# Attention, a routed MoE and a dense layer in one kernel: squares and gate work moved to other places in the queues, two buffers of local queries and keys

## The chip, the cores and the metric

One core of a Trainium2 chip runs the whole program. Its engines work through queues of their own, strictly in order: TensorE (PE in the profile, its weight loads PEld), VectorE (DVE), ScalarE (ACT), GpSimd (POOL), and SyncE (SP), which issues most DMAs. An instruction that waits for another engine holds up everything behind it in its own queue. The metric is device time in microseconds (us); three runs of the kernel before took 641.94, 642.94 and 644.06, and 642.94 is their median.

## The reference, cut to what matters

Attention over 4 batches, 8 heads, 576 positions and 64 channels, then a mixture of 8 experts on the 2304 rows, then a dense layer with three up-projections and their maximum.

```python
# heads 0..3: local (0 <= rel < 32); heads 4..7: strided (same position modulo 32, rel >= 0)
scores = np.where(masks, scale * q @ k.T, -1e9)
attn = np.exp(scores - scores.max(-1)); attn /= attn.sum(-1) + 1e-9
x = (attn @ v) as rows of 512
xn = x / (norm(x) + 1e-6); en = emb / (norm(emb) + 1e-6)
logits = xn @ en.T / tau
expert_idx = argmax(logits)
gate_w = softmax(logits)[expert_idx]
out[mask] = gate_w[mask] * (relu(x[mask] @ w1[e]) @ w2[e])      # for each expert e
h = max(x @ w1, x @ w2, x @ w3); return h @ w_out
```

The expert of a row follows from the products with the normed embeddings alone, so it can be found without the norm of the row. The norm enters only in the gate weight, which is multiplied in at the very end of the kernel.

## The kernel before, in words

The program has an attention stage, then the experts one after the other, then the dense layer in blocks of 768 rows. The change touches the attention stage and its hand-over to the first expert.

**Steps of attention.** A batch is cut into six groups (`GRP`): k = 0, 1, 2 are strided heads (8, 8 and 6 softmax columns), k = 3, 4, 5 are local heads (8, 8 and 2 columns). The loop in `attention` runs over steps s; step s masks and scores group s, takes maximum and exponentials of group s-1, normalises group s-2, transposes group s-3 and multiplies group s-4 by V. So the step after a group with k = 5 has 2 exponentials and the others have 6 or 8. For a group: `g_max` (L390 on VectorE, and L394, the scaled negative maximum `nb`, on GpSimd), `g_exp` (L405, one ACTIVATE for each column on ScalarE), `g_sum` (L414, GpSimd), `g_norm` (reciprocal `ri` L420 on VectorE, then the multiplication of `p` L421 on GpSimd), `g_trans` (transposes L432, copy `pt`), `g_av` (product `x` L457 into the one PSUM buffer `x`, whose copy `xt` is put into the list `later` and emitted at the start of the next step, on ScalarE for strided and on VectorE for local heads). `tok_half` (L492) turns `xt` into rows of 128 tokens, copies them (`row`) and writes them to `x_scr`.

**Routing of a unit of tokens.** The 18 tiles of 128 tokens are routed in units of 4, 5, 4, 2 and 3 tiles. `route_stages` gives each unit's stages: `square` (L530, one ScalarE instruction for each tile: sum of squares), `logits` (VectorE, which expert), `rank` (TensorE) and `slots`, `onehots`, `tokens`, `sums` (VectorE, place in the expert's list), and `norm` (GpSimd, L546 and L547), `gate` and `gate2` (softmax of the logits: two GpSimd instructions, an exponential `pr` on ScalarE, small VectorE work). The stages go through the list `todo`, from which up to TP = 4 are emitted at the end of each step. The last unit runs `order`, which counts, sorts the experts by load and forms `win_i`, the row numbers that each expert gathers. The stages of the last two units that only the gate needs are emitted after `order` (the list `late`).

**Hand-over.** `gather(0)` (L833) is emitted after all of attention: three indirect DMAs on GpSimd fetch the rows of the first expert from `x_scr`. Two weight tiles are then split on ScalarE and VectorE (L168, L173), the gathered rows are transposed on TensorE (L862), split (`xw`, L844 and L845), and the first expert's products start (L869).

**Queues.** SyncE issues the loads of queries, keys and values of the next batch (`load_kq`, `load_v`) at fixed steps, the writes to `x_scr`, and the first two pieces `c` of the dense layer's weights (`c_load`, at steps S0 and S0 + 1). Local queries and keys (`ql`, `kl`) have one buffer.

Of the kernel before, what the change touches and what calls it, by code (L numbers as in the profile page):

```python
# [9 lines left out]
F32 = mybir.dt.float32  # L10
# [12 lines left out]
SCALE = 0.125  # L23
# [8 lines left out]
CA = 0  # L32
S0 = 13
NSTAGE = 3
NMORE = 40
CL = 0
CS = 1
E1 = 2
NA = 4
# [14 lines left out]
PSR = 2  # L54
TP = 4
W0 = 4
# [8 lines left out]
def kernel(ctx, tc, a, out, x_scr, w_scr, u_scr, perm_scr, gate_scr, upto="all"):  # L65
# [218 lines left out]
    v_p = actx.enter_context(tc.tile_pool(name="v", bufs=2))  # L284
    p_p = actx.enter_context(tc.tile_pool(name="p", bufs=LT + 1))
    pt_p = actx.enter_context(tc.tile_pool(name="pt", bufs=LA - LT + 3))
    st_p = actx.enter_context(tc.tile_pool(name="st", bufs=LA + 3))
# [31 lines left out]
    def load_kq(b, kind, cuts=None):  # L319

        for n0, n1 in cuts or ((0, S),):
            if kind:
                for t, x in zip(qk_s[::-1], ("kts", "qs")):
                    nc.sync.dma_start(
                        out=t[b % 2][:, 0:2 * S].rearrange("p (c n) -> p c n", c=2)[:, :, n0:n1], in_=a[x][b][:, :, n0:n1])
            else:
                nc.sync.dma_start(out=kl, in_=a["ktl"][b])
                nc.sync.dma_start(out=ql, in_=a["ql"][b])

# [18 lines left out]
    st = {}  # L348
    later, later_v = [], []

# [15 lines left out]
    def g_scores(g):  # L366

        b, kind, bl = group(g)  # L370
        ps, (ns, nk) = st[g]["ps"], shape(g)
        for i in range(ns):
            blk, c = bl[i // 2], i % 2
            for u in range(1 if kind else 2):
                for h in range(2):
                    r = slice(64 * h, 64 * h + 64)
                    if kind:
                        o = S * c + 54 * blk
                        q, k, p0 = qk_s[0][b % 2][r, o:o + 64], qk_s[1][b % 2][r, o:o + 54], 64 * h
                    else:  # L380
                        o = 64 * blk + 32 * u
                        q, k, p0 = ql[r, c, o:o + 32], kl[r, c, o:o + 64], 64 * u + 32 * h
                    nc.tensor.matmul(  # L383
                        out=ps[p0:p0 + q.shape[-1], nk * i:nk * i + nk], lhsT=q, rhs=k, start=False, stop=i == ns - 1,
                        skip_group_check=True)

    def g_max(g):
# [54 lines left out]
    def g_av(g):  # L442
# [38 lines left out]
    def tok_half(i, kind):  # L481
# [15 lines left out]
        if q not in rows:  # L497
            rows[q] = row_p.tile([128, 3 if q == 4 else 5, 4, 136], F32, tag=f"row{q // 4}", name="row", bufs=2 - q // 4)
        dst = rows[q][:, i - t0, 2 * kind:2 * kind + 2, :]
# [16 lines left out]
    def route_stages(b):  # L516
# [61 lines left out]
        def tokens():  # L578
# [88 lines left out]

        sq = [(0, lambda t=t: square(t)) for t in range(T)]
        if b < 3:
            return (sq[:-1] + [(0, logits)] + sq[-1:] + [(0, norm), (1, rank), (0, gate), (0, slots), (0, gate2), (0, onehots)]  # L670
                    + [(1, tokens), (0, sums)])
        rest = sq + [(0, f) for f in (norm, gate, gate2)]
        if b == 3:
            late.extend(rest)
            return [(0, f) for f in (logits, rank, sums, slots, onehots, tokens)]
        return [(0, f) for f in (logits, order)] + late + rest

    def setup():
# [5 lines left out]
        for t in qk_s[0] + qk_s[1]:  # L684
            nc.gpsimd.memset(t[:, 2 * S:NP], 0.0)
        for i in range(LT + 1):
            nc.gpsimd.memset(new_p()[:, :, 54:64], 0.0)
# [32 lines left out]

    late = []

    def attention():
        toks, todo = [], []
        last, seen, routed = [0], [0], [0]

        def next_tok():
            if toks:
                f = toks.pop(0)
                f()  # L730

        for s in range(NG + LA + 1):
# [6 lines left out]
            if 0 <= s - 1 < NG:  # L739
                g_max(s - 1)  # L740
                g_exp(s - 1)
            if 0 <= s - LN < NG:
                g_norm(s - LN)
# [9 lines left out]
            if 0 <= s - LA < NG:  # L753
# [5 lines left out]
                while k >= NS and 128 * seen[0] + 128 <= end:  # L759
# [3 lines left out]
                    if seen[0] == t0 + T:  # L763
                        toks.append(lambda q=routed[0]: todo.extend(route_stages(q)))
                        routed[0] += 1
# [4 lines left out]
            if s < NG:  # L770
                b, k = divmod(s, NB_)
                if b + 1 < B:
                    if k == 0:
                        load_kq(b + 1, 1)
                    if k == 2:
                        load_v(b + 1, 1)
                    if k == 4:
                        load_v(b + 1, 0)
                    if k == 5:
                        load_kq(b + 1, 0)  # L780
            if s in (S0, S0 + 1):
                c_load()
            if 4 < s < NG:
                now[0] += 4500
                c_after()
                if c_n[0] < CA:
                    c_before()
            for _ in range(TP):
                if todo and s >= last[0] + todo[0][0]:
                    todo.pop(0)[1]()  # L790
                    last[0] = s
        while toks:
            next_tok()
            flush(later_v)
        while todo:
            todo.pop(0)[1]()

# [22 lines left out]
    yt = [yt_p.tile([128, YT], F32, name=f"yt{c}") for c in range(4)]  # L820
    xg, xw, hh_t = {}, {}, {}

    def wins(e):
        return [(i, min(128, CAPS[e] - 128 * i)) for i in range(-(-CAPS[e] // 128))]

    def gather(e):
        t = xg_p.tile([128, 3, DM], F32, tag="xg", name="xg")
        t = [t[:, i, :] for i in range(3)]
        if len(wins(e)) > 3:
            assert e == 0  # L830
            t.append(h_p.tile([128, 2 * HB], F32, tag="h7", name="x3")[:, 0:DM])
        for i, r in wins(e):
            nc.gpsimd.indirect_dma_start(  # L833
                out=t[i][:r], out_offset=None, in_=x_scr,
                in_offset=bass.IndirectOffsetOnAxis(ap=win_i[:r, NWIN * e + i:NWIN * e + i + 1], axis=0))
        xg[e] = t

    def xw_tiles(n):
# [204 lines left out]

    gather(0)
    usable[0] = NRING
# [377 lines left out]
```

## Time and profile before

| What | us |
|---|---|
| median of three runs | 642.94 |
| the profiled execution, its own time | 647.8 |
| span of its trace | 646.0 |
| start of the first expert's products | 139.58 |
| PE busy in the span | 601.2 (93%) |
| DVE, ACT, POOL busy | 417.2, 323.5, 133.3 |

Up to 139.58 the trace is attention, routing and the hand-over; all that follows is the same in both kernels. A share of busy time over the whole span says little on this first part: there the slices of the profile have PE at 4 to 8 tenths, with its granted clock (PEclk) between 4 and 9 tenths of full speed. TensorE has two clock levels, 1.2 and 2.4 GHz; a granted clock of 0.50 in a stretch is the lower, 1.00 the higher.

### The profile page before, as it was taken

How to read it: one execution, taken by the hardware profiler on the slowest of the kernel's cores; microseconds unless marked ns; L12 is line 12 of the kernel's file. 1: busy time of each engine (PE TensorE's matmuls, PEld its weight loads, DVE VectorE, ACT ScalarE, POOL GpSimd, SP SyncE). 2: the span in 40 equal slices, each digit the busy share in tenths (PEclk: the TensorE clock that was granted, in tenths of full speed). 3: DMA queues.
4: the chain of work that ended last, by engine and by line, in shares of the span. 5: the costliest groups of instructions: out<-in, count | busy, mean ns of one | idle time of the engine just before them, and what ended most of it. 6: DMA issues, size and time to landing. Idle time of an engine off the chain costs nothing.

```text
span 646.0 us, 13803 instructions
## 1 busy us (share of the span) xinstructions
PE 601.2 (93%) x5320; PEld 564.0 (87%) x5321; DVE 417.2 (65%) x885; ACT 323.5 (50%) x905; POOL 133.3 (21%) x183
## 2 busy tenths in 40 slices
PE   7878886679999999999998999999999999999995
PEld 5767775469999999999998999988999988999984
DVE  2556574446989797979898878777354376334440
ACT  4684764234756567656765634536412246221242
POOL 2343432247414241422210000002100002000011
PEclk8787898579999999999999899999999999999998
DMA  8955721266797786868775685951177301367111
GB/s 292 381 193 211 233 68 48 101 212 205 243 355 264 259 278 245 299 207 274 266 241 179 256 330 180 333 221 66 56 268 266 126 17 66 135 252 268 47 50 53
DMA packets 44183, 129.93 MB, mean 201 GB/s; under 512 B 4400, under 2 KB 15024, under 8 KB 40912
## 3 DMA queue, kind: packets, MB, share of 16 engines
q1 hardware_dynamic: 41088, 119.50, 52.3%
q0 software_dynamic: 3024, 9.49, 4.0%
q8 instruction: 44, 0.72, 0.5%
q14 instruction: 27, 0.22, 0.1%
HBM read 96.73 MB, written 32.24 MB: 200 GB/s over the span
## 4 chain that ended last, share of the span: by engine, by line
PE 79%; DVE 7%; ACT 5%; DMA 5%; issue 2%; SPq 1%; POOL 1%; POOLq 0%; DVEq 0%; ACTq 0%
PE g L869 57%; PE q L869 10%; PE r L492 3%; PE x L457 2%; PE s L383 2%; ACT p L405 2%; DMA stage<-w 2%; ACT junk L530 1%; PE q L852 1%; DMA em<-emb 1%; DVE w L173 1%; DMA out<-r,perm_i 1%; PE t L432 1%; DVE h L889 1%; DMA xg<-x_scr,win_i 1%
## 5 line engine op out<-in xcount | busy, mean ns | idle before, releaser
L869 PE MATMUL g<-xc,w 128*128 128x384 f32 x1134 | 198.0, 335 | 0.0
L869 PEld LDWEIGHTS g<-xc,w 128*128 128x128 f32 x1134 | 196.5, 188 | 1.2 <-ACT yt L1167 0.5
L173 DVE TENSOR_TENSOR w<-stage,w 128x1024 fp32r<-128x1024 f32 x76 | 104.7, 1394 | 16.2 <-ACT w L168 15.8
L869 PE MATMUL g<-h,w 128*128 128x376 f32 (+7 forms) x768 | 113.6, 304 | 1.6 <-DVE h L889 1.6
L869 PEld LDWEIGHTS g<-h,w 128*128 128x128 f32 x768 | 106.4, 192 | 2.8 <-DVE h L889 2.2
L869 PE MATMUL g<-xw,w 128*128 128x376 f32 (+7 forms) x768 | 106.0, 298 | 0.4 <-ACT xw L844 0.3
L869 PEld LDWEIGHTS g<-xw,w 128*128 128x128 f32 x768 | 104.3, 189 | 0.9 <-ACT xw L844 0.5
L168 ACT ACTIVATE w<-stage 128x1024 fp32r<-128x1024 f32 x76 | 78.6, 1055 | 5.4 <-DMA stage<-w 4.7
L1218 POOL DMA_INDIRECT out<-r,perm_i x18 | 18.2, 1010 | 281.5 <-ACT r L1217 186.1
L869 PE MATMUL q<-w,hs 128*128 128x512 f32 x324 | 74.9, 391 | 1.3 <-DVE hs L1206 1.3
L869 PEld LDWEIGHTS q<-w,hs 128*128 128x128 f32 x324 | 60.6, 188 | 14.8 <-DVE hs L1206 2.6
L405 ACT ACTIVATE p<-s,nb 128x54 f32<-128x54 f32 (+1 forms) x160 | 46.9, 317 | 30.8 <-POOL nb L394 30.8
L244 POOL TENSOR_TENSOR f<-f,c 128x512 int32<-128x512 int32 x24 | 34.9, 1456 | 108.6 <-DVE f L242 97.1
L1167 ACT ACTIVATE yt<-g 128x384 f32<-128x384 f32 x27 | 13.3, 491 | 72.8 <-PE g L869 47.3
L1154 DVE TENSOR_TENSOR tmp<-g,yt 128x384 f32<-128x384 f32 x36 | 20.0, 556 | 44.7 <-PE g L869 44.7
L888 ACT ACTIVATE h<-g 128x376 fp32r<-128x376 f32 (+7 forms) x64 | 25.7, 411 | 29.8 <-PE g L869 27.6
L405 ACT ACTIVATION_READ_ACCUMULATOR p<-s,nb 128x1 f32 x160 | 34.2, 214 | 0.0
L903 ACT ACTIVATE yt<-g 128x376 f32<-128x376 f32 (+7 forms) x32 | 13.2, 413 | 38.7 <-PE g L869 38.7
L1007 DVE TENSOR_TENSOR xc<-yt,xc 128x384 fp32r<-128x384 f32 x42 | 21.4, 554 | 16.5 <-ACT xc L1006 16.5
L457 PEld LDWEIGHTS x<-pt,v 64*64 64x64 f32 (+2 forms) x928 | 17.4, 147 | 16.4 <-ACT xt L468 12.3
L457 PE MATMUL x<-pt,v 64*64 64x32 f32 (+2 forms) x928 | 20.4, 234 | 12.0 <-ACT xt L468 10.6
L833 POOL DMA_INDIRECT xg<-x_scr,win_i x22 | 26.0, 1181 | 24.8 <-PE q L983 11.5
(181 smaller groups left out, 725.8 us busy)
## 6 DMA issues: line engine op xcount, KB each, us to landing
stage<-w SPq DMA_DIRECT2D x64, 512.0 KB, 5.2
c<-wm SPq DMA_DIRECT2D x24, 512.0 KB, 6.2
w<-u_scr SPq DMA_DIRECT2D x12, 1024.0 KB, 4.8
u_scr<-w SPq DMA_DIRECT2D x9, 1024.0 KB, 7.7
w<-u_scr SPq DMA_DIRECT2D x12, 768.0 KB, 6.5
u_scr<-w SPq DMA_DIRECT2D x9, 768.0 KB, 10.1
w_scr<-f SPq DMA_DIRECT2D x24, 256.0 KB, 5.2
stage<-w_scr SPq DMA_DIRECT2D x12, 512.0 KB, 4.3
```

The costliest lines, as they stand in the source:

```text
L168: nc.scalar.activation(out=ws[i][:, 0, 0:m], in_=x, func=ACTF.Copy)
L173: nc.vector.tensor_tensor(out=ws[i][:, 1, 0:m], in0=x, in1=ws[i][:, 0, 0:m].bitcast(F32), op=ALU.subtract)
L244: nc.gpsimd.tensor_tensor(out=f, in0=f, in1=low, op=ALU.add)
L405: nc.scalar.activation(out=p[:, i, :nk], in_=st[g]["ps"][:, i * nk:(i + 1) * nk], func=ACTF.Exp, bias=st[g]["nb"][:, i:i + 1], scale=SCALE ...
L457: nc.tensor.matmul(out=xp[64 * h:64 * h + 64, c, o:o + n], lhsT=lhsT, rhs=rhs, start=True, stop=True)
L492: nc.tensor.matmul(out=psv[p0:p0 + n, c, :], lhsT=xT[b, kind][:, c, off:off + n], rhs=rhs_i[:, 2 * kind + c, :], start=True, stop=True)
L833: nc.gpsimd.indirect_dma_start(out=t[i][:r], out_offset=None, in_=x_scr, in_offset=bass.IndirectOffsetOnAxis(ap=win_i[:r, NWIN * e + i:NWI ...
L869: nc.tensor.matmul(out=ps, lhsT=ws(i), rhs=xs(j), start=first and n == 0, stop=last and n == 2, skip_group_check=more)
L888: nc.scalar.activation(out=h[:, 0], in_=ps, func=ACTF.Relu)
L1007: nc.vector.tensor_tensor(out=x[:, 1], in0=src[c], in1=x[:, 0].bitcast(F32), op=ALU.subtract)
L1154: nc.vector.tensor_tensor(out=tmps[i], in0=ps, in1=s, op=ALU.add)
L1218: nc.gpsimd.indirect_dma_start(out=out, out_offset=bass.IndirectOffsetOnAxis(ap=perm_i[:, col:col + 1], axis=0), in_=r, in_offset=None)
```

## The change

- The unit list becomes 4, 5, 4 and 5 tiles.
- `square` leaves `todo`. It goes into a new list `aside`, from which squares are emitted only at the end of steps with s modulo 6 equal to 0 (three), 2 (one) and 3 (two), and only while s < 24. `norm`, `gate` and `gate2` follow there one per step. `todo` gives one stage per step.
- `gather(0)` is emitted inside `attention`, after the stages in `todo` and ahead of what is left in `aside`: four squares, norm, gate and gate2 of the third unit, five squares and the same of the fourth.
- `nb`, both instructions of `gate` (df) and `tokens`' product w_tok move from GpSimd to VectorE.
- `xt` copies of local heads are emitted behind the maximum, `nb` and exponentials of the step (list `later_d`).
- `ql` and `kl` get two buffers and are loaded at k = 1 in place of k = 5; strided values at k = 1 in place of k = 2. `p` has three buffers (was 4) and `pt` three (was 4).
- The first two `c` loads are emitted at steps 20 and 21 (was 13 and 14); the embedding's norm one step later.

```diff
-S0 = 13
+S0 = 20
-E1 = 2
+E1 = 3
-TP = 4
+TP = 1
...
-    ql = pa.tile([128, 2, S], F32, name="ql")
-    kl = pa.tile([128, 2, S + 32], F32, name="kl")
+    qk_l = [[pa.tile([128, 2, n], F32, name=f"{x}{u}") for u in range(2)] for x, n in (("ql", S), ("kl", S + 32))]
...
-        nc.gpsimd.tensor_scalar(out=nb[:, 0:ns], in0=mx[:, 0:ns], scalar1=SCALE, scalar2=None, op0=ALU.mult)
+        nc.vector.tensor_scalar(out=nb[:, 0:ns], in0=mx[:, 0:ns], scalar1=SCALE, scalar2=None, op0=ALU.mult)
...
-            later.append(lambda: nc.vector.tensor_copy(out=dst, in_=src))
+            later_d.append(lambda: nc.vector.tensor_copy(out=dst, in_=src))
...
-    units = ((0, 4), (4, 5), (9, 4), (13, 2), (15, 3))
+    units = ((0, 4), (4, 5), (9, 4), (13, 5))
...
-            (nc.gpsimd if b < 4 else nc.vector).tensor_tensor(
+            nc.vector.tensor_tensor(
                 out=w_tok[:, t0:t0 + T], in0=bc(bt.unsqueeze(2), n4), in1=bc(tk.unsqueeze(3), n4), op=ALU.mult)
...
-            nc.gpsimd.tensor_tensor(out=df, in0=d["l"], in1=bc(d["mx"], s8), op=ALU.subtract)
-            nc.gpsimd.tensor_tensor(out=df, in0=df, in1=bc(rn, s8), op=ALU.mult)
+            nc.vector.tensor_tensor(out=df, in0=d["l"], in1=bc(d["mx"], s8), op=ALU.subtract)
+            nc.vector.tensor_tensor(out=df, in0=df, in1=bc(rn, s8), op=ALU.mult)
...
-        sq = [(0, lambda t=t: square(t)) for t in range(T)]
-        if b < 3:
-            return (sq[:-1] + [(0, logits)] + sq[-1:] + [(0, norm), (1, rank), (0, gate), (0, slots), (0, gate2), (0, onehots)]
-                    + [(1, tokens), (0, sums)])
-        rest = sq + [(0, f) for f in (norm, gate, gate2)]
-        if b == 3:
-            late.extend(rest)
-            return [(0, f) for f in (logits, rank, sums, slots, onehots, tokens)]
-        return [(0, f) for f in (logits, order)] + late + rest
+        sq = [lambda t=t: square(t) for t in range(T)]
+        if b < B - 1:
+            return [logits, lambda: (rank(), slots()), onehots, lambda: (tokens(), sums())], sq, [norm, gate, gate2]
+        return [logits, order], sq, [norm, gate, gate2]
...
+    SQ = {0: 3, 2: 1, 3: 2}
...
+        def route(q):
+            now_, squares, gates = route_stages(q)
+            todo.extend(now_)
+            aside.extend([(1, f) for f in squares] + [(0, f) for f in gates])
...
-            for _ in range(TP):
-                if todo and s >= last[0] + todo[0][0]:
-                    todo.pop(0)[1]()
-                    last[0] = s
+            if aside and not aside[0][0]:
+                aside.pop(0)[1]()
+            elif s < NG:
+                for _ in range(SQ.get(s % NB_, 0)):
+                    if aside and aside[0][0]:
+                        aside.pop(0)[1]()
+            if todo and routed[0] < B:
+                todo.pop(0)()
         while toks:
             next_tok()
             flush(later_v)
-        while todo:
-            todo.pop(0)[1]()
+        for f in todo:
+            f()
+        gather(0)
+        for _, f in aside:
+            f()
```

**ScalarE, end of batch 2 and start of batch 3** (p: exponentials of a group's columns; xt: copy of the product with V; junk: a square). Before:

```order
L405 ACTIVATE p,rs<-s,nb 128x64 x8
L468 ACTIVATE xt<-x 128x36x12
L405 ACTIVATE p,rs<-s,nb 128x64 x2
L530 ACTIVATE junk,ssq<-row 128x512 x4
L468 ACTIVATE xt<-x 128x36x8
L405 ACTIVATE p,rs<-s,nb 128x54 x8
L530 ACTIVATE junk,ssq<-row 128x512
```

Now, at the same place:

```order
L404 ACTIVATE p,rs<-s,nb 128x64 x8
L467 ACTIVATE xt<-x 128x36x12
L404 ACTIVATE p,rs<-s,nb 128x64 x2
L529 ACTIVATE junk,ssq<-row 128x512 x3
L467 ACTIVATE xt<-x 128x36x8
L404 ACTIVATE p,rs<-s,nb 128x54 x16
L529 ACTIVATE junk,ssq<-row 128x512
```

Three squares in place of four stand ahead of the batch's third xt copy, and the fourth stands two groups of exponentials later instead of one.

**ScalarE, from the last xt copy of attention to the first expert** (pr: the gate's exponential; w: upper half of a weight tile; xw: upper half of the gathered rows). Before:

```order
L465 ACTIVATE xt<-x 128x64
L502 ACTIVATE row<-r 128x272
L530 ACTIVATE junk,ssq<-row 128x512 x2
L591 ACTIVATE pr<-df 128x16
L530 ACTIVATE junk,ssq<-row 128x512 x3
L591 ACTIVATE pr<-df 128x24
L168 ACTIVATE w<-stage 128x1024 x2
L844 ACTIVATE xw<-g 128x376 x4
```

Now:

```order
L464 ACTIVATE xt<-x 128x64
L529 ACTIVATE junk,ssq<-row 128x512 x4
L590 ACTIVATE pr<-df 128x32
L529 ACTIVATE junk,ssq<-row 128x512 x5
L590 ACTIVATE pr<-df 128x40
L168 ACTIVATE w<-stage 128x1024 x2
L847 ACTIVATE xw<-g 128x376 x4
```

Nine squares stand here in place of five, still ahead of the first weight split, and each pr still stands between them.

**GpSimd, the same stretch** (r: sums plus 1e-9; xg: an indirect DMA of the gather; nrm and nr: the norm). Before:

```order
L583 TENSOR_TENSOR w_tok<-bt,cf 128x96
L546 TENSOR_TENSOR nrm<-ssq,ca 128x2
L547 TENSOR_SCALAR nr_2298<-nrm 128x2
L589 TENSOR_TENSOR df<-l,mx 128x16
L590 TENSOR_TENSOR df<-df,rn 128x16
L546 TENSOR_TENSOR nrm<-ssq,ca 128x3
L547 TENSOR_SCALAR nr_2318<-nrm 128x3
L589 TENSOR_TENSOR df<-l,mx 128x24
L590 TENSOR_TENSOR df<-df,rn 128x24
L833 DMA xg<-x_scr,win_i 128x512 x2
L833 DMA xg<-x_scr,win_i 120x512
```

Now:

```order
L420 TENSOR_TENSOR p<-p,ri 128x128
L725 DMA xg<-x_scr,win_i 128x512 x2
L725 DMA xg<-x_scr,win_i 120x512
L545 TENSOR_TENSOR nrm<-ssq,ca 128x4
L546 TENSOR_SCALAR nr_2257<-nrm 128x4
L545 TENSOR_TENSOR nrm<-ssq,ca 128x5
L546 TENSOR_SCALAR nr_2279<-nrm 128x5
```

The three gathers now stand ahead of both norms, and the norms behind the gathers.

## Rows read from the trace of the kernel before

**Rows 1.** Busy time by stage: start:end, length, each engine (instructions), PEclk, DMA, GB/s.

```profile
22.55:42.22 19.67, 19.45 (x524) 17.30 (x524) 12.79 (x33) 12.53 (x77) 7.38 (x18) 0.86 0.65 233
42.22:70.11 27.89, 22.56 (x550) 19.33 (x544) 15.94 (x49) 16.84 (x99) 10.36 (x24) 0.82 0.64 230
70.11:95.41 25.30, 20.53 (x534) 18.10 (x530) 16.31 (x51) 16.73 (x95) 10.32 (x23) 0.87 0.46 153
95.41:117.05 21.64, 14.06 (x233) 11.21 (x234) 9.15 (x37) 9.96 (x37) 4.38 (x10) 0.76 0.16 48
117.05:139.58 22.53, 13.06 (x79) 9.76 (x78) 10.12 (x46) 5.51 (x14) 7.05 (x16) 0.63 0.38 127
139.58:646.00 506.42, 495.70 (x3087) 476.24 (x3087) 347.00 (x656) 248.76 (x515) 86.25 (x66) 0.99 0.58 205
```

**Rows 2.** Waits from 15 to 110 us: total, times, longest.

```profile
ACT p L405 <- POOL nb L394: 26.7, 18, 3.9
PE x L457 <- ACT xt L468: 10.6, 6, 3.4
```

**Rows 3.** Timeline around a batch's end: start, us, instruction, [idle before <-releaser].

```profile
72.62 0.62 ACT L530 ACTIVATE junk<-row 128x512 f32<-128x512 f32 x1
...
75.51 0.39 ACT L468 ACTIVATE xt<-x 128x288 f32<-128x288 f32 x1
...
75.95 2.18 PE L492 MATMUL r<-rhs_i,xt 128*128 128x136 f32 x8 [1.91 <-ACT xt L468]
...
78.53 0.43 DVE L536 TENSOR_REDUCE l<-row 128x40 f32<-128x160 f32 x1
...
78.88 1.20 POOL L546 TENSOR_TENSOR nrm<-ssq,ca 128x5 f32<-128x5 f32 x1 [4.22 <-ACT junk L530]
...
79.92 0.20 DVE L542 TENSOR_TENSOR oh_all<-v,vm 128x40 bf16<-128x40 f32 x1
```

**Rows 4.** Busy time by stage, five microseconds after a wait of TensorE.

```profile
46.69:51.69 5.00, 5.00 (x70) 4.08 (x70) 1.37 (x3) 2.84 (x17) 2.31 (x6) 0.50 1.02 410
```

**Rows 5.** Timeline of the third group's maximum and nb.

```profile
11.78 0.50 DVE L390 TENSOR_REDUCE mx<-s 128x6 f32<-128x324 f32 x1 [0.65 <-PE s L383]
...
14.18 0.25 POOL L394 TENSOR_SCALAR nb<-mx 128x6 f32<-128x6 f32 x1
```

**Rows 6.** Timeline from the end of attention to the first expert.

```profile
99.33 0.88 PE L457 MATMUL x<-pt,v 54*64 54x54 f32 x24 [3.27 <-ACT xt L468]
...
113.45 0.20 PE L554 MATMUL rk<-oh_all,cb 128*128 128x16 bf16 x1 [2.58 <-DVE oh_all L542]
...
116.61 0.44 DVE L504 COPY row<-r 128x272 f32<-128x272 f32 x1 [3.21 <-PE r L492]
...
123.15 0.18 DVE L663 TENSOR_REDUCE win_i<-wp 128x3 int32<-128x24 f32 x1
...
128.71 0.22 ACT L591 ACTIVATE pr<-df 128x24 f32<-128x24 f32 x1 [1.91 <-POOL df L590]
128.84 1.99 ACT L168 ACTIVATE w<-stage 128x1024 fp32r<-128x1024 f32 x2
...
129.54 1.24 POOL L833 DMA_INDIRECT xg<-x_scr,win_i  x1 [0.86 <-issue]
...
132.36 1.00 POOL L833 DMA_INDIRECT xg<-x_scr,win_i  x1 [0.30 <-issue]
...
138.46 1.61 ACT L844 ACTIVATE xw<-g 128x376 fp32r<-128x376 f32 x4 [7.63 <-PE g L862]
```

**Rows 7.** Timeline: small VectorE work beside a GpSimd instruction, and without one.

```profile
111.66 0.51 POOL L583 TENSOR_TENSOR w_tok<-bt,cf 128x192 bf16<-128x192 f32 x1 [5.31 <-DVE bt L580]
111.73 0.46 DVE L606 TENSOR_TENSOR coh<-coh,ohs 128x8 bf16<-128x8 bf16 x1
...
117.16 0.17 DVE L606 TENSOR_TENSOR coh<-coh,ohs 128x8 bf16<-128x8 bf16 x1
```

**Rows 8.** Instructions by line, 0 to 110 us: count, busy, mean ns, idle before.

```profile
L421 POOL TENSOR_TENSOR p<-p,ri 128x432 f32<-128x432 f32 (+3 forms) x24 | 20.1, 839 | 0.8 <-DVE ri L420 0.3
```

More of the change, by code (lines that the diff above doesn't have):

```diff
@@ L284 @@
     v_p = actx.enter_context(tc.tile_pool(name="v", bufs=2))
-    p_p = actx.enter_context(tc.tile_pool(name="p", bufs=LT + 1))
-    pt_p = actx.enter_context(tc.tile_pool(name="pt", bufs=LA - LT + 3))
+    p_p = actx.enter_context(tc.tile_pool(name="p", bufs=LT))
+    pt_p = actx.enter_context(tc.tile_pool(name="pt", bufs=LA - LT + 2))
     st_p = actx.enter_context(tc.tile_pool(name="st", bufs=LA + 3))
@@ L326, in load_kq @@
             else:
-                nc.sync.dma_start(out=kl, in_=a["ktl"][b])
-                nc.sync.dma_start(out=ql, in_=a["ql"][b])
+                for t, x in zip(qk_l[::-1], ("ktl", "ql")):
+                    nc.sync.dma_start(out=t[b % 2], in_=a[x][b])
     def load_v(b, kind):
@@ L348 @@
     st = {}
-    later, later_v = [], []
+    later, later_d, later_v = [], [], []
     def flush(fs):
@@ L381, in g_scores @@
                         o = 64 * blk + 32 * u
-                        q, k, p0 = ql[r, c, o:o + 32], kl[r, c, o:o + 64], 64 * u + 32 * h
+                        q, k, p0 = qk_l[0][b % 2][r, c, o:o + 32], qk_l[1][b % 2][r, c, o:o + 64], 64 * u + 32 * h
                     nc.tensor.matmul(
@@ L497, in tok_half @@
         if q not in rows:
-            rows[q] = row_p.tile([128, 3 if q == 4 else 5, 4, 136], F32, tag=f"row{q // 4}", name="row", bufs=2 - q // 4)
+            rows[q] = row_p.tile([128, 5, 4, 136], F32, tag="row", name="row")
         dst = rows[q][:, i - t0, 2 * kind:2 * kind + 2, :]
@@ L685, in setup @@
             nc.gpsimd.memset(t[:, 2 * S:NP], 0.0)
-        for i in range(LT + 1):
+        for i in range(LT):
             nc.gpsimd.memset(new_p()[:, :, 54:64], 0.0)
@@ L719, in embed3, with wins, gather @@
         nc.vector.tensor_copy(out=rhs_i[:, :, 0:128], in_=bc(ident.unsqueeze(1), [128, 4, 128]))
-    late = []
+    xg, xw, hh_t = {}, {}, {}
+    def wins(e):
+        return [(i, min(128, CAPS[e] - 128 * i)) for i in range(-(-CAPS[e] // 128))]
+    def gather(e):
+        t = xg_p.tile([128, 3, DM], F32, tag="xg", name="xg")
+        t = [t[:, i, :] for i in range(3)]
+        assert len(wins(e)) <= 3
+        for i, r in wins(e):
+            nc.gpsimd.indirect_dma_start(
+                out=t[i][:r], out_offset=None, in_=x_scr,
+                in_offset=bass.IndirectOffsetOnAxis(ap=win_i[:r, NWIN * e + i:NWIN * e + i + 1], axis=0))
+        xg[e] = t
+    SQ = {0: 3, 2: 1, 3: 2}
     def attention():
-        toks, todo = [], []
-        last, seen, routed = [0], [0], [0]
+        toks, todo, aside = [], [], []
+        seen, routed = [0], [0]
         def next_tok():
             if toks:
-                f = toks.pop(0)
-                f()
+                toks.pop(0)()
+        def route(q):
+            now_, squares, gates = route_stages(q)
+            todo.extend(now_)
+            aside.extend([(1, f) for f in squares] + [(0, f) for f in gates])
         for s in range(NG + LA + 1):
@@ L741, in attention @@
                 g_exp(s - 1)
+            flush(later_d)
             if 0 <= s - LN < NG:
@@ L763, in attention @@
                     if seen[0] == t0 + T:
-                        toks.append(lambda q=routed[0]: todo.extend(route_stages(q)))
+                        toks.append(lambda q=routed[0]: route(q))
                         routed[0] += 1
@@ L774, in attention @@
                         load_kq(b + 1, 1)
-                    if k == 2:
+                    if k == 1:
+                        load_kq(b + 1, 0)
                         load_v(b + 1, 1)
@@ L778, in attention @@
                         load_v(b + 1, 0)
-                    if k == 5:
-                        load_kq(b + 1, 0)
             if s in (S0, S0 + 1):
@@ L820 @@
     yt = [yt_p.tile([128, YT], F32, name=f"yt{c}") for c in range(4)]
[L821 to L836, printed above, removed]
     def xw_tiles(n):
@@ L1041 @@
     perm_todo += [lambda i=i: perm_part(i) for i in range(NPT)]
-    gather(0)
     usable[0] = NRING
```

## The prediction

> **What bounds the kernel now.** I read the busy times by stage first, because the page's shares mix stages with different limits. The last stage, from 139.58 on, has TensorE busy 495.70 of 506.42 us at clock 0.99 [rows 1]; the order of instructions there is the same in both kernels, so I leave it as it is, and the question is only when it starts. Of the four batches of attention the second (22.55 to 42.22) has no routing beside it: 19.67 us, TensorE busy 19.45. The third and fourth carry the routing of the units before them and take 27.89 and 25.30, with TensorE busy 22.56 and 20.53. So a step of attention is bound by TensorE when nothing disturbs it, and routing costs 8.2 and 5.6 us a batch.
>
> Next I read the waits, for what disturbs it: ScalarE's exponentials wait 26.7 us for `nb` from GpSimd, and TensorE's product x waits 10.6 us for the xt copy on ScalarE, 3.4 at the longest [rows 2]. The timeline shows how that arises: four squares run from 72.62 until the third strided copy starts at 75.51, 0.72 us each, and TensorE stands 1.91 us at 75.95 until it has ended [rows 3]. Such a wait costs more than itself. The five microseconds after another one (46.69 to 51.69) have a granted clock of 0.50, the lower level, with TensorE busy throughout [rows 4]; at the upper level the same work would take half, so a wait of this kind costs about 2.5 us on top.
>
> Last I read the hand-over. The last row copy ends at 116.61 + 0.44 = 117.05, which I call T. The first expert's window is known at 123.33 (T + 6.28), but the first gather starts only at 129.54, because GpSimd's queue holds both norms and df ahead of it, and these wait for squares. The third gather starts at 132.36, and the xw split at 138.46; the experts start at T + 22.5 [rows 1, 6].
>
> **The change, part by part.** All against the profiled execution: 647.8 us, span 646.0 and 1.8 around it. That is 4.9 above the median of the runs, which I take off at the end.
>
> *nb on VectorE.* Removed: 24 instructions on GpSimd and, more important, their place in its queue behind r, which waits for the exponentials of the group before. The third group's maximum ended at 12.28 and its nb started at 14.18 [rows 5], so ScalarE lost 1.9 us there. Behind the maximum on VectorE nb follows at once; I price it like the smallest VectorE instruction shown, 0.17 us [rows 7], 4 us over 24 groups. It is hidden where TensorE bounds (VectorE is busy 12.79 of 19.67 in the undisturbed batch). In the first two batches I take a gain of 2 us, one such stall; the ends are 0 (TensorE or the loads bound instead) and 4 (two).
>
> *Squares, routing and xt copies.* In the third and fourth batch three squares, not four, stand ahead of the third xt copy (2.2 us instead of 2.9), behind two exponentials that no longer wait for GpSimd. I lay the engines side by side for that place: logits on VectorE (1.59 us from 78.53 to the end of oh_all [rows 3]) hold up the maximum behind them, so the two exponentials and the three squares end about 1.3 us after TensorE could use the copy. A batch is then 19.67, plus this 1.3, plus about 1 us for the step in which VectorE has onehots or tokens on top of its maximum, copies and rows: 22. The 19.67 holds one stretch at the lower clock already (mean 0.86). Two batches at 22 against 27.89 + 25.30 give 9.2. Bounds: 19.7 each (13.8 gained), and 25 each, near the faster of the two as they are (3.2 gained). I take 22, nearer to the undisturbed batch, as the squares are what TensorE waited for.
>
> *The rest of attention, 95.41 to T: 21.64 us, TensorE busy 14.06 at clock 0.76* [rows 1]. Gone: the 3.27 us in which x at 99.33 waits for a copy behind squares (those of the third unit now run after T), and the 2.58 us in which the rank of the unit of two tiles waits for VectorE at 113.45, ahead of the last two row products [rows 6]. Its clock share says that about half of the 14.06 ran at the lower level, so TensorE's work is 11 us if it stays warm, and it still waits for copies of x and rows, some 2.6 us. That makes 13.6, a gain of 8; bounds 5 (only the two waits go) and 10 (no wait left).
>
> *T to the experts.* The unit of two tiles no longer stands between T and `order`, but the last unit has five tiles: logits as above 1.59 us, and more rows in the one-hots. I get the first window at T + 5.65, 0.6 earlier. The gathers start there, at about T + 6.0. But ScalarE's queue has two pr ahead of the weight splits, and these now hang on norms that stand behind the gathers. Counted on: three gathers until T + 9.8 (129.54 to 133.36 took 3.8); norm of four tiles 1.4; three small VectorE instructions 0.7; pr 0.2, so T + 12.1. Then five squares at 0.75: T + 15.85. The norm of five tiles (1.20 and its second instruction, 1.55 in all [rows 3]): T + 17.4. VectorE 0.7, pr 0.2: T + 18.3. Two weight splits on ScalarE, 1.99 [rows 6]: T + 20.3; VectorE follows them, then the split of xw: the experts start at T + 22.3. The gather comes more than 6 us earlier and the start 0.2. Four of the nine squares are hidden (they run while GpSimd waits for the window); the other five are not. And TensorE, which before had transposes and warming products until just before the start, now has nothing from about T + 14.6 until T + 20.8, and starts cold: 2.5 us by the price above, bounds 0 and 4.
>
> *The rest at nothing.* The second buffer of local queries and keys frees SyncE's queue, but no wait of TensorE for a load stands among the waits that I read; if the loads come in a worse order early, it costs up to 1 us in the first batch. Fewer p and pt buffers: the transposes that free them come ahead of the scores that the next exponentials need. The c loads move within a stretch where DMA is at 0.16 to 0.46 [rows 1], and are used long after. df and w_tok on VectorE: within the microsecond above.
>
> Sum: 2 + 9.2 + 8 + 0.2 - 2.5 = 16.9. 647.8 - 16.9 = 630.9; less 4.9, 626.
>
> **A rule against the change.** coh, a VectorE instruction on 8 columns, takes 0.46 us beside w_tok on GpSimd, which it outlasts by a hair, and 0.17 with GpSimd idle [rows 7]. So a small VectorE instruction can be held until GpSimd is done. The Trainium skill, SBUF — State Buffer, section "SBUF: two separate sides", says that the two share one port pair, which whoever comes first keeps for a whole instruction; by that rule, and the rows agree, nb, df and w_tok can be held on VectorE.
>
> **Rivals.**
>
> *The gather ends last (617).* If the gate chain were hidden, the experts would start as they do now after the third gather: 6.1 us from it to xw [rows 6] and 1.1 more, so T + 6.0 + 2.8 + 7.2 = T + 16.0, and warm. That is 9 us earlier. Against it: the order puts both pr ahead of the weight splits. Chance 0.08.
>
> *The stalls only move (637).* VectorE becomes the bound of a step, batches stay at 25 and the rest of attention gains 5: 0 + 3.2 + 5 + 0.2 - 2.5 = 5.9. For it: VectorE is busy 16.31 of 25.30 and gets nb and df on top; against it: its time was not what TensorE waited for. Chance 0.21.
>
> *Nothing that can be measured (641 to 645, that is within 0.3%, about what tells a change from none here).* The attention gains little and the cold start takes it back. Chance 0.04.
>
> *Slower (652): the xt copy of local heads behind maximum and nb.* TensorE's product needs the one x buffer; the copy now starts some 0.9 us later. If TensorE waits over a microsecond for it, the lower clock follows as above. Nine copies at 0.9 + 2 are 26 us, against 16.9 gained. It decides from about six such waits on. Against it: mask, transposes and row products stand between in TensorE's queue. Chance 0.03.
>
> *Slower by held nb (651).* If each of 24 nb waited out GpSimd's product with p, 0.84 us on average [rows 8], with that instruction's copies behind it, some 25 us come back. That product is emitted behind the reciprocal and so behind the nb of its step, and should have ended a step later. This is what the rule of the Trainium skill would make of it. Chance 0.02.
>
> **How the numbers follow.** Forecast 0.62, at 626, by itself 620 to 633. The range 617 to 637 adds the early gather and the moved stalls up to their value. Faster by over 0.3%: 0.62 + 0.08 + 0.21 = 0.91; within 0.3% 0.04; slower 0.05.
>
> **What would show it.** Right: no ScalarE wait for nb over 2 us; squares behind two exponentials and batches of about 22 us; the experts start near 120 us (139.58 less 19.4), with the last gather landed some 9 us before; in ScalarE's queue norm, five squares, norm and pr just ahead of the first weight split; the lower clock in the first microseconds of the experts. Wrong: batches of 25 us, VectorE never idle in them, or x waiting for xt on VectorE; or an experts' stage that is not 506 us long.

## The result, and the profile after

The changed kernel takes 636.07 us (median of 13 runs, 634.11 to 641.13); the kernel before took 644.06 beside it (641.9 to 647.56). The ratio is 0.9881, 95% interval 0.9856 to 0.9905: faster by 8.0 us. The forecast was 626, so 16.9 from the median of 642.94. The time lies inside the range, 10 us above the forecast.

The profiled execution after took 634.37 us, its span is 632.5. Here are the busy times by stage after, cut where the rows of before were cut [rows 1]: second, third and fourth batch, rest of attention up to the last row copy (T), hand-over, experts and dense layer. Columns: stretch and length, then busy time and count of PE, PEld, DVE, ACT and POOL, granted clock, DMA share, GB/s.

```profile
20.20:42.98 22.78, 19.89 (x535) 17.49 (x528) 13.22 (x37) 13.12 (x83) 6.02 (x12) 0.93 0.78 295
42.98:67.24 24.26, 19.68 (x550) 16.63 (x544) 17.59 (x60) 17.36 (x102) 8.62 (x15) 1.00 0.63 224
67.24:88.26 21.02, 17.49 (x536) 15.28 (x530) 16.99 (x55) 16.50 (x94) 8.00 (x15) 1.00 0.52 168
88.26:104.03 15.77, 12.43 (x231) 10.28 (x232) 9.32 (x35) 6.90 (x27) 1.91 (x4) 0.89 0.17 50
104.03:125.93 21.90, 11.15 (x83) 8.35 (x82) 10.07 (x42) 8.87 (x23) 9.67 (x13) 0.78 0.48 164
125.93:632.50 506.57, 496.25 (x3087) 476.40 (x3087) 346.09 (x656) 247.77 (x513) 82.23 (x64) 0.99 0.57 204
```

T comes 13.0 us earlier than in [rows 1], and the experts start 13.65 earlier: nearly all of the gain lies in the attention, and the hand-over (21.90 against 22.53) and the rest (506.57 against 506.42) are about as long as before. So the spans of the two profiled executions differ by 13.5 us and the medians by 8.0. That gap of 5.5 is the first thing to explain.

The chain of the hand-over after, from its timeline (start, length, engine, line, operation; in brackets the idle time before and what ended it), to be held against [rows 6]:

```profile
103.59 0.44 DVE L503 COPY row<-r 128x272 f32<-128x272 f32 x1 [0.59 <-PE r L491]
109.52 0.18 DVE L662 TENSOR_REDUCE win_i<-wp 128x3 int32<-128x24 f32 x1
110.00 1.24 POOL L725 DMA_INDIRECT xg<-x_scr,win_i  x1 [16.68 <-DVE wp L658]
115.77 0.23 ACT L590 ACTIVATE pr<-df 128x32 f32<-128x32 f32 x1 [10.16 <-DVE df L589]
115.91 0.61 ACT L529 ACTIVATE junk<-row 128x512 f32<-128x512 f32 x1
119.72 1.19 POOL L545 TENSOR_TENSOR nrm<-ssq,ca 128x5 f32<-128x5 f32 x1 [4.49 <-ACT junk L529]
121.84 0.24 ACT L590 ACTIVATE pr<-df 128x40 f32<-128x40 f32 x1 [2.20 <-DVE df L589]
121.98 1.99 ACT L168 ACTIVATE w<-stage 128x1024 fp32r<-128x1024 f32 x2
117.38 0.57 PE L865 MATMUL g<-cf,xg 120*128 120x120 f32 x4
124.39 0.68 PE L872 MATMUL g<-xw,w 128*128 128x376 f32 x1 [6.44 <-ACT xw L847]
```

The gather starts at T + 6.0, the last transposes are over at 117.95, and then TensorE waits 6.44 us for the split of xw. That split stands behind the weight splits in ScalarE's queue, and these stand behind the second pr; ScalarE had idled 10.16 us ahead of the first pr.

### The profile page after: what moved, and what is told of

Its sections match the earlier page's. It is cut to its first block, busy times and chain, and to the rows that moved or that the text cites. A ratio compares the mean times of both kernels' runs of the same rounds, so it can differ in the third digit from the quotient of the medians.

```text
span 632.5 us, 13808 instructions
## 1 busy us (share of the span) xinstructions
PE 594.1 (94%) x5321; PEld 557.6 (88%) x5322; DVE 419.8 (66%) x901; ACT 322.7 (51%) x904; POOL 122.0 (19%) x142
## 4 chain that ended last, share of the span: by engine, by line
PE 83%; DVE 7%; ACT 4%; issue 2%; DMA 2%; POOL 1%; POOLq 0%; DVEq 0%; ACTq 0%
PE g L872 61%; PE q L872 10%; PE s L382 3%; PE r L491 3%; PE x L456 2%; ACT p L404 2%; PE q L855 1%; ACT junk L529 1%; DMA out<-r,perm_i 1%; PE t L431 1%; DMA stage<-w 1%; DVE mx L389 1%; DVE w L173 1%; PE warm L513 1%; DVE tmp L1156 1%
## 5 line engine op out<-in xcount | busy, mean ns | idle before, releaser
L872 PE MATMUL g<-xw,w 128*128 128x376 f32 (+7 forms) x768 | 108.1, 301 | 7.3 <-ACT xw L847 6.4
L872 PE MATMUL g<-h,w 128*128 128x376 f32 (+7 forms) x768 | 112.0, 302 | 1.6 <-DVE h L892 1.6
L872 PEld LDWEIGHTS g<-xw,w 128*128 128x128 f32 x768 | 106.2, 191 | 7.9 <-ACT xw L847 6.7
L872 PEld LDWEIGHTS g<-h,w 128*128 128x128 f32 x768 | 104.8, 189 | 2.9 <-DVE h L892 2.2
L404 ACT ACTIVATE p<-s,nb 128x54 f32<-128x54 f32 (+1 forms) x160 | 47.0, 321 | 25.0 <-DVE nb L393 18.3
L892 DVE SCALAR_TENSOR_TENSOR h<-g,h 128x376 fp32r<-128x376 f32 (+7 forms) x64 | 27.1, 450 | 6.9 <-ACT h L891 6.9
L491 PE MATMUL r<-rhs_i,xt 128*128 128x136 f32 (+1 forms) x160 | 23.6, 307 | 3.7 <-ACT xt L467 1.5
```

The costliest lines, as they stand in the source:

```text
L404: nc.scalar.activation(out=p[:, i, :nk], in_=st[g]["ps"][:, i * nk:(i + 1) * nk], func=ACTF.Exp, bias=st[g]["nb"][:, i:i + 1], scale=SCALE ...
L491: nc.tensor.matmul(out=psv[p0:p0 + n, c, :], lhsT=xT[b, kind][:, c, off:off + n], rhs=rhs_i[:, 2 * kind + c, :], start=True, stop=True)
L872: nc.tensor.matmul(out=ps, lhsT=ws(i), rhs=xs(j), start=first and n == 0, stop=last and n == 2, skip_group_check=more)
L892: nc.vector.scalar_tensor_tensor(out=h[:, 1], in0=ps, scalar=0.0, in1=h[:, 0].bitcast(F32), op0=ALU.max, op1=ALU.subtract)
```

## The experiments

Each is an edit of the changed kernel (636.07, and 634.31 in a later run), but for the first. Ratios are to the kernel before, run beside it, with their 95% intervals. The two runs of the changed kernel differ by 1.8 us, so a difference of that size to either of them tells nothing.

**The kernel before, once more.**

> The kernel before, unchanged, profiled a second time. Theory: the miss of the prediction lies mostly in the last subtraction. The first profiled execution took 647.8 us against a median of 642.9 because TensorE spent more of its attention at the lower clock than usual (clock shares 0.82 to 0.87 in the second to fourth batch); so the excess was part of what the change removes and was counted twice. Then a second profile has a span of 641 to 643 us, and 3 to 5 us of the difference lie between 20 and 117 us of the span, with the experts' stage again 506 to 508 us long. Rival: the excess lies in the experts' stage or is spread over all of it; then the attention takes the same 117 us up to the last row copy, and the stage of the experts is shorter by 4.

Median 644.01 (ratio 1.0001, 0.9969 to 1.0033); the profiled execution took 643.62, so it is an ordinary one. Its busy times by stage, cut as above:

```profile
23.53:43.48 19.95, 19.71 (x524) 17.60 (x524) 12.84 (x33) 12.25 (x76) 7.41 (x18) 0.84 0.66 226
43.48:69.13 25.65, 21.29 (x549) 18.30 (x544) 15.30 (x49) 16.44 (x95) 10.14 (x24) 0.87 0.66 242
69.13:92.23 23.10, 17.70 (x535) 15.26 (x530) 16.33 (x52) 17.25 (x98) 10.68 (x24) 1.00 0.51 171
92.23:114.05 21.82, 14.20 (x233) 11.36 (x234) 9.15 (x37) 9.99 (x37) 4.39 (x10) 0.79 0.16 47
114.05:137.24 23.19, 12.76 (x79) 9.54 (x78) 10.11 (x46) 5.52 (x14) 7.07 (x16) 0.68 0.39 129
137.24:641.90 504.66, 494.00 (x3087) 474.55 (x3087) 346.58 (x656) 248.63 (x515) 85.76 (x66) 1.00 0.58 205
```

The third and fourth batch take 48.75 us here and 53.19 in [rows 1]: 4.44 less, with the clock at 0.87 and 1.00 instead of 0.82 and 0.87. Of these 4.44, 4.10 are busy time of TensorE (38.99 against 43.09) for the same 1084 products. The span differs by 4.1; the experts' part is shorter by 1.8, the first batch and the hand-over longer. From the second batch to the last row copy it is 90.52 us here and 94.50 in [rows 1]. My theory, 3 to 5 us in this part, held, with 1.8 of the rival's beside it: the experts' stage, expected at 506 to 508, took 504.66.

**Reordered end** (tail). All squares and the first norm ahead of the gather:

```diff
+        gates = [f for k, f in aside if not k]
-        for f in todo:
+        for f in [f for k, f in aside if k] + gates[:1] + todo:
             f()
         gather(0)
-        for _, f in aside:
+        for f in gates[1:]:
             f()
```

> The changed kernel, with all squares and the norm of the last but one unit ahead of the gather, the rest of the gate work behind it. Theory: what sets the experts' start is the chain pr, five squares, norm, pr ahead of the weight splits on ScalarE; with the five squares at 105.6 to 109.4 us the second pr ends near 116.3 and the experts start at 118.5 to 120 instead of 124.4 and 125.9, with TensorE idle for under 2 us before: 5 to 7 us against the changed kernel, 629 to 631 median. Rival: the stage of the experts is bound by its loads at the start, or the gathers and transposes come later, and less than 2 us come through.

Median 629.82 (0.9793, 0.9765 to 0.9821), 6.3 us below the changed kernel and 4.5 below its later run. The end of that chain in its timeline:

```profile
109.93 0.63 ACT L529 ACTIVATE junk<-row 128x512 f32<-128x512 f32 x1
117.17 0.24 ACT L590 ACTIVATE pr<-df 128x40 f32<-128x40 f32 x1 [4.95 <-DVE df L589]
117.32 1.99 ACT L168 ACTIVATE w<-stage 128x1024 fp32r<-128x1024 f32 x2
119.00 0.57 PE L866 MATMUL g<-cf,xg 120*128 120x120 f32 x4
119.90 0.44 PE L873 MATMUL g<-xw,w 128*128 128x376 f32 x1 [0.33 <-ACT xw L848]
```

T is 105.24 here, so the splits start at T + 12.1 instead of T + 17.95, and TensorE waits 0.33 instead of 6.44. From T to the experts (121.27) it takes 16.0 us instead of 21.9. The theory held in place, and in size within that spread.

**Squares all at once** (sq_all), at the step at which they come up: `-SQ = {0: 3, 2: 1, 3: 2}`, `+SQ = {k: 5 for k in range(NB_)}`.

> The changed kernel, with the squares of a unit all run at the step at which they come up, as in the kernel before, and not three, one and two at set steps. Forecast theory: squares ahead of the xt copies are what TensorE waits for in the third and fourth batch; undone, these get 5 to 8 us longer together, TensorE's longest wait for xt on ScalarE rises from 1.1 to over 2.5 us, and the median rises to 640 to 643. Rival: the step of attention is bound by the round through all engines, and ScalarE has room: under 2 us more, 636 to 638.

Median 635.01 (0.9857, 0.9827 to 0.9888): no loss. By that number the rival wins, but its reason is wrong, as the stages show:

```profile
43.20:68.44 25.24, 20.28 (x550) 17.62 (x544) 17.17 (x61) 17.42 (x101) 8.56 (x15) 0.86 0.57 206
68.44:92.92 24.48, 19.22 (x536) 16.72 (x530) 17.31 (x60) 16.90 (x95) 8.20 (x15) 0.93 0.49 153
92.92:111.74 18.82, 13.43 (x231) 11.17 (x232) 8.72 (x34) 9.73 (x35) 3.18 (x6) 0.82 0.11 33
111.74:127.77 16.03, 10.97 (x82) 8.28 (x82) 9.06 (x35) 5.87 (x14) 6.51 (x9) 0.79 0.61 206
```

T is 7.7 us later (4.4 of it in the two batches, 3.05 in the rest), and the hand-over is 5.9 us shorter, with only one unit's squares and gate left behind T. TensorE's waits for the xt copy on ScalarE between 43 and 112 us (total, times, longest) are, here:

```profile
PE x L456 <- ACT xt L467: 8.7, 4, 3.9
```

and after the change:

```profile
PE x L456 <- ACT xt L467: 3.0, 4, 1.1
```

Set steps move work past T: what the attention gains, the hand-over pays.

**Both together** (sq_all_tail).

> Squares all at once (as in the run of that name) and the reordered end (as in the run of that name), together; it closes a square of four kernels: changed 636.1, squares all at once 635.0, reordered end 629.8. Theory: set steps for the squares bring the last row copy forward by 7.7 us (111.7 to 104.0), but leave nine squares and two gates to stand behind it, which takes back 6 to 7 us before the experts; with the end reordered nothing is taken back. Then the reordered end gives nothing here, where one unit's squares alone are left behind the last row copy: last row copy near 111.5, experts at 126, median 634 to 636. Rival: the set steps are worth nothing in themselves and the reordered end alone gains: then about 629.

Median 632.79 (0.9818, 0.9793 to 0.9844), between the two: 2.2 below sq_all, 3.0 above tail. T is at 110.01 and the experts start 14.30 us later, at 124.31: 3.0 later than with tail. By the medians, set steps gain 3.0 with the end in order and nothing without (-1.1), and the reordered end gives 2.2 here where the theory had nothing. By the ratios the two differences are 1.6 and 2.5, and the intervals overlap, so the direction is likely and not shown.

**Gates ahead of the gather** (gates_ahead): `gather(0)` behind the loop over `aside`.

> The changed kernel, with the squares, norms and gates of the last two units emitted ahead of the first expert's gather (behind the order of the experts, as in the kernel before) and not behind it. Theory: what the early gather wins waits for the gate chain on ScalarE, so the order of these two is a trade: gather near 116 instead of 110 us, but both pr and the weight splits over by 119, the last transposes near 124; the experts start within 1.5 us of now (124.4 and 125.9), and TensorE has transposes shortly before and starts at the upper clock: 634 to 637 median. Rival: the early gather is worth its 6 us; then the median rises to 640 or more.

Median 635.6 (0.9869, 0.9843 to 0.9895), in the theory's range. From its timeline:

```profile
117.12 1.23 POOL L725 DMA_INDIRECT xg<-x_scr,win_i  x1 [0.86 <-DVE df L589]
116.83 0.24 ACT L590 ACTIVATE pr<-df 128x40 f32<-128x40 f32 x1 [2.18 <-DVE df L589]
127.71 2.57 PE L872 MATMUL g<-xw,w 128*128 128x376 f32 x11 [0.33 <-ACT xw L847]
```

The gather is 7.1 us later than after the change, both pr are over by 117.07, and the products of the first expert run from 127.71, at clock 1.00 in the first 4 us, instead of one at 124.39 and the rest from 125.93 at 0.50. The start is later than the theory's 1.5 us. The time is the same: the early gather alone is worth nothing, the gate chain must go out of the way too.

**nb back on GpSimd** (nb_gpsimd): `nc.gpsimd.tensor_scalar(out=nb...`.

> The changed kernel, with nb back on GpSimd and all else as changed. Forecast theory: nb on VectorE is worth 2 us in the first two batches (0 to 4); undone, the median rises to 638 (636 to 640), and ScalarE waits for nb again in the first 20 us. Rival one: it is worth much more, since squares and exponentials are spaced by it in the later batches: above 641. Rival two: on VectorE it is held by GpSimd's products and holds up what is behind it, so that undoing it gains: 633 to 635.

Median 635.55 (0.9874, 0.9849 to 0.99): nothing, below the forecast's 2. ScalarE waits for nb as ever, and it costs nothing. The row of its waits between 15 and 105 us (waiting engine and line, releaser, us, times, longest):

```profile
ACT p L404 <- POOL nb L393: 21.1, 18, 3.3
```

and the one after the change, where the same stretch is waited for on VectorE:

```profile
ACT p L404 <- DVE nb L393: 15.0, 8, 2.8
```

**xt copies of local heads ahead of the maximum** (xt_ahead): `later_d.append` becomes `later.append`.

> The changed kernel, with VectorE's copy of a local head's x put back ahead of the maximum (where the kernel before has it). Theory: behind maximum and nb this copy makes r and x wait on TensorE (0.38, 0.86 and 1.14 us seen) and holds up the reciprocal and GpSimd's product by 0.7 us a step; putting it back gives 2 to 4 us against the changed kernel: 632 to 634 median. Rival: the copy then holds up the maximum and the exponentials by the same 0.7 us, and the time stays within 1 us of 636, or is worse by 1 to 3.

Median 633.17 (0.9831, 0.9806 to 0.9856), 2.9 under the one run of the changed kernel and 1.1 under the other. TensorE's longest wait for that copy falls from 1.1 to 0.4, but T is no earlier in the profiled execution (104.74). The intervals touch, so this is a gain of 1 to 3 us at most, and where it arises isn't shown. **With the reordered end** (xt_tail):

> The changed kernel with two edits at once: VectorE's copy of a local head's x ahead of the maximum, and all squares and the first norm ahead of the gather. One by one they gave 633.2 and 629.8. Theory: they act in different places (inside the batches, and between the last row copy and the experts), so the gains of 2.9 and 6.3 add up: 626 to 628. Rival: the first was worth nothing, and its lower median comes from how often an execution falls to the lower clock; then 629 to 630.

627.2 (0.9738, 0.971 to 0.9766): 2.6 under tail alone, as the theory has it, though the intervals touch here too. This is the best kernel of all, 16 us under the kernel before.

**Loads as before** (loads_before): `range(2)` of `qk_l` becomes `range(1)] * 2`, `load_v(b + 1, 1)` at k == 2, `load_kq(b + 1, 0)` at k == 5.

> The changed kernel, with one buffer of local queries and keys and the loads of a batch issued at the steps of the kernel before (short values at the third step, local keys and queries at the sixth). Theory: in every profile of the changed kernel and its variants the second batch takes 22.3 to 22.8 us instead of 19.7 to 20.0, with DMA busy 0.78 to 0.81 instead of 0.65 and TensorE standing inside groups of products where nothing that the trace shows is waited for; the earlier loads are the cause. Then the second batch falls to 19.7 to 20.5 us here, TensorE's stalls at 28 and 34 us go, and the median falls by 1 to 3 us, to 633 to 635. Rival: the second batch starts 2 us earlier and only meets the same arrival of data; then it ends at the same 43 us, and the median stays at 636 or rises by up to 2, since local heads of the next batch wait for their load.

638.04 (0.9912, 0.9881 to 0.9943), 2.0 and 3.7 above the two runs of the changed kernel; the second batch still takes 22.76. The theory fell; the earlier loads with the second buffer are worth 0 to 4 us.

**df and w_tok back on GpSimd** (small_gpsimd).

> The changed kernel, with df and (in all units but the last) w_tok back on GpSimd, as in the kernel before. Theory: they are hidden on VectorE but for the instructions that GpSimd's product holds (0.87 and 0.52 us instead of 0.16 and 0.17), under 1 us in all; the median stays within 1 us of 636. Rival one: VectorE is relieved of what holds up its maximum, and the time falls by 2 or more. Rival two: on GpSimd the df of the last units stands behind the gathers and norms and the weight splits start later: 1 to 2 us slower.

635.51 (0.9875, 0.9847 to 0.9903): nothing, as the theory has it. The hold itself is real. After the change, from the timeline:

```profile
87.16 1.04 POOL L420 TENSOR_TENSOR p<-p,ri 128x512 f32<-128x512 f32 x1 [0.39 <-DVE ri L419]
87.38 0.87 DVE L588 TENSOR_TENSOR df<-l,mx 128x40 f32<-128x40 f32 x1
115.36 0.16 DVE L588 TENSOR_TENSOR df<-l,mx 128x32 f32<-128x32 f32 x1
121.39 0.18 DVE L588 TENSOR_TENSOR df<-l,mx 128x40 f32<-128x40 f32 x1
```

The first df ends when GpSimd's product does; away from that product the same size takes 0.18 us. The Trainium skill, SBUF — State Buffer, section "SBUF: two separate sides", says that the two engines share a port pair, held for a whole instruction; these rows agree. The run says what it costs here: nothing that can be measured.

**Masks three times** (masks3): `in list(enumerate(parts)) * 3`.

> The changed kernel, with the products that lay the masks into the scores' sums run three times over in each step (each time from an empty sum, so the scores are the same): 0.4 to 1.1 us more of TensorE in each of 24 steps, some 17 us at the upper clock level. Forecast theory: an undisturbed step is bound by TensorE; then nearly all 17 us show, and the median is 650 to 655. Theory now: the third and fourth batch are bound by the round through all engines, since they take as long at a mean granted clock of 0.86 (21.48 us of products in 23.57 us) as at 1.00 (19.68 in 24.26); a step's round has the mask ahead of the scores in it, but the other products of TensorE wait beside it; then under 8 us show: 638 to 644.

638.39 (0.9899, 0.9858 to 0.9941): 2.3 to 4.1 more. My 17 us were too many: TensorE's busy time for these products between 20 and 105 us rose from 6.3 to 11.3 us. So the number alone does not decide. The third batch says more:

```profile
44.24:67.30 23.06, 21.10 (x563) 17.53 (x558) 16.80 (x57) 16.46 (x95) 7.97 (x15) 1.00 0.64 231
```

TensorE has 1.4 us more work than in the changed kernel at the same clock, and the batch is 1.2 shorter: TensorE's work alone did not set the 24.26. What did stays open: the batch also starts 1.26 us later here, and ends at 67.30 as against 67.24.

**The changed kernel, once more** (after_again), and two on the second batch: four buffers for p (p_four, `bufs=LT + 1`) and the embedding a step earlier (e1_two, `E1 = 2`).

> The changed kernel, unchanged, profiled a second time. Theory: its executions differ by how long TensorE is at the lower clock between 20 and 105 us, and most of all in the last stretch before the last row copy; expected: batches of 22.3 to 22.8, 23.5 to 25.4 and 20.5 to 22, last row copy at 104 to 110 us, from there 21 to 22 us to the experts in every case, and the experts' stage within 1 us of 506.5. Rival: executions differ in the experts' stage by more than 2 us.

> The changed kernel, with four buffers for the exponentials p (as in the kernel before) and not three. Theory: with three, a group's exponentials wait until the transposes of the group three before are done; in the second batch, where nothing of the routing runs, the changed kernel takes 22.3 to 22.8 us and the kernel before 19.7 to 20.0. If this buffer is the reason, the second batch falls below 21 us and the median by 1 to 3 us, to 632 to 634 (the changed kernel had 636.1 and 634.3). Rival: the transposes are over long before, as the forecast said; then the second batch stays at 22 to 23 us and the median at 634 to 636.

> The changed kernel, with the normed embedding (its transposes on TensorE and its copies on VectorE) one step earlier, where the kernel before has it. Theory: these 0.4 to 0.6 us of TensorE and 1 us of VectorE have moved from the first batch into the second, so that the first is shorter by about 2 us and the second longer by as much; undone, the mark between the batches moves back towards 22 us and the end of the second stays at 42 to 43.5, with the median at 634 to 636. Rival: the later embedding holds up the second batch's chain for more than its own length; then the second batch ends before 41 us and the median falls by 1 to 2.

after_again: 634.31 (0.9843, 0.9813 to 0.9874); its batches take 22.46, 24.01 and 21.24, T is 103.97, hand-over 21.89, the experts and all behind them 505.94. All that is close to what was expected. Its third and fourth batch:

```profile
42.42:66.43 24.01, 19.46 (x550) 16.50 (x544) 17.36 (x60) 17.19 (x101) 8.38 (x15) 1.00 0.63 226
66.43:87.67 21.24, 17.73 (x535) 15.36 (x529) 17.16 (x55) 16.71 (x96) 8.23 (x15) 1.00 0.52 166
```

p_four: 635.31 (0.9874, 0.983 to 0.9917), e1_two: 636.69 (0.9888, 0.9848 to 0.9928); the second batch takes 22.38 and 23.16. Neither is the cause. What makes it longer than 20 us once it starts earlier stays open: in all these kernels it ends at 41.9 to 44.8.

Undone one at a time, no part of the change gives back more than 2 to 4 of the 8 us. The new list of units, one routing stage a step, the three buffers of pt and the later c loads were not undone. Which of them the rest of the gain needs is not shown.

## Why the prediction missed, step by step

- **"Less 4.9" for an execution above the median: wrong, and the largest part.** The forecast treated those 4.9 us as lying outside the change. They lay inside it: the third and fourth batch of that execution were 4.44 us longer than in the one ordinary execution profiled. The sum took that as gain, and then took it off once more. Of the 10 us between 626 and 636.07, 4.9 are this step, 3.4 are the sum itself (16.9 against 13.5 between the two executions), and 1.7 are that the profiled execution after lay under its own median. On the ordinary pair, before_again and after_again, the spans differ by 10.1, not 16.9: 1.1 up to the end of the second batch, 3.5 in batches 3 and 4, 5.5 in the rest of attention, 1.3 in the hand-over and -1.3 behind it.
- **Batches 3 and 4, 9.2: mis-sized.** Against the first execution it was 7.9 (53.19 to 45.28), against the ordinary one 3.5 (48.75 to 45.25). The place was right: undone, the squares give 4.4 back. The target of 22 rested on 19.67 as the length of a batch that TensorE bounds. No profile after the change shows that: the third batch takes 23.6 to 24.3 us with set steps (25.3 in loads_before, 23.1 in masks3), as long with the clock at 0.86 (tail, below) as at 1.00 (19.68 busy of 24.26, above):

```profile
43.51:67.08 23.57, 21.48 (x550) 18.41 (x544) 17.25 (x60) 17.20 (x100) 8.53 (x15) 0.86 0.61 221
```

In this batch of the changed kernel the lower clock filled idle time, and did not cost the 2.5 us that I put on every stall. In the kernel before it did go with a longer batch, 2.2 us in the third and in the fourth.

- **Rest of attention, 8: mis-sized.** 5.9 against the first execution, 5.5 against the ordinary one. The wait of the rank is gone, and that of x for the copy is down from 3.27 to 1.07; the clock is 0.89, and TensorE still idles 3.3 us. sq_all keeps 3 of it, so set steps make half; what makes the other half was not separated.
- **nb, 2: wrong.** Undone, nothing changes beyond 1.3 us either way: ScalarE's waits for nb are idle time that nobody waits for. The second batch ends at 42.22 and 43.48 in the two executions before, and at 42.98 and 42.42 in those after. That no wait would be over 2 us was wrong as well (2.8).
- **T to the experts, 0.2: right, row by row.** Gather T + 6.0 as forecast; weight splits T + 17.95 for T + 18.3; start T + 21.9 for T + 22.3; last gather landed by 117.38, 8.5 us before. The gain in the hand-over is 0.6, and 1.3 on the ordinary pair.
- **Cold start, 2.5: near, 1.7 at most.** The first four microseconds of the experts after the change:

```profile
125.93:129.93 4.00, 4.00 (x13) 4.00 (x14) 1.31 (x3) 0.03 (x1) 0.40 (x1) 0.50 0.90 348
```

and before:

```profile
139.58:143.58 4.00, 4.00 (x23) 4.00 (x24) 2.16 (x5) 1.93 (x4) 2.79 (x3) 1.00 0.83 305
```

13 products instead of 23: ten products at the upper level (4.00 us for 23) are 1.7 us. With the end reordered the first 4 us hold 23 again, at 1.00. The stage as a whole shows less: 505.83 us with the reordered end against 506.57 after the change.

- **Terms put at nothing.** df and w_tok were nothing. The loads with the second buffer are 0 to 4 us in favour of the change. The longer second batch (22.78 for 19.67) was in no term; it starts earlier by nearly as much.

Of the rivals, "the stalls only move" has the right number, 637, for another reason: batches did not stay at 25 (24.3 and 21.0). The gather that ends last (617) is what the reordered end comes to: 4.5 to 6.3 of its 9 us. The local heads' xt copy behind the maximum did make TensorE wait, once by 1.1 us in the trace; that is a price of 1 to 3 us, not of 26.

## What to carry to other kernels

Before a sum is made against one profiled execution, profile the kernel a second time: time that one execution spent at the lower clock must not be counted as what the change saves, and a difference to the median can't be taken off a sum that already holds it. A wait counts only with whoever waits for the waiting engine: ScalarE's waits for nb, 15 us or 21, made no difference, while the 6.44 us that TensorE stood in front of the experts were worth 4.5 to 6.3. And work moved out of a loop is paid where it lands: the set steps won 7.7 us in the attention and gave back 5.9 behind it, in one profiled execution of each kernel.

## What was not expected of the hardware

Ten executions of the kernel before lie between 641.94 and 649.75 us, and the mean granted clock goes with them: 0.967 at 641.94, 0.949 at 649.75. In the third batch of the changed kernel the clock level hardly shows in the time (above). Ahead of the last row copy it goes with the time: masks3 has 0.61 in this stretch, the changed kernel 0.89 in its own of 15.77 us.

```profile
88.00:109.76 21.76, 17.79 (x255) 15.01 (x248) 10.69 (x38) 8.18 (x35) 2.95 (x5) 0.61 0.19 56
```

Of the 6.0 us more, 5.4 are busy time of TensorE (17.79 against 12.43). What made the clock fall there was not tested.
